# SyncE's queue and the order of seven products in a gated-attention kernel with a feed-forward layer

## The chip, the cores and the metric

The kernel runs on one core of a Trainium2 chip, in one launch. The metric is the device time in microseconds; the numbers below are medians of repeated runs. The engines are called as the profile calls them: PE (TensorE), PEld (its weight loads), DVE (VectorE), ACT (ScalarE), POOL (GpSimd), SP (SyncE). SP computes nothing here; it issues nearly all DMA transfers, one after the other.

## The reference

Two blocks follow each other. The first is attention with a complex gate per step, run as a recurrence over 768 steps for 4 batches of 8 heads of width 48; the second is a feed-forward layer over the 3072 resulting rows of 384 numbers.

```python
scale = np.minimum(mag, 0.999) / (mag + 1e-06)        # mag = |a_re + i a_im|
for t in range(S):
    new_re = ar * S_re - ai * S_im                     # ar, ai: the scaled gate of step t
    new_im = ar * S_im + ai * S_re
    S_re, S_im = new_re + k_t v_t^T, new_im
    y[:, :, t] = q_t S_re
x = y as 3072 x 384
h = x @ w_in                                           # 384 x 2048
out = (h * cos(h)) @ w_out                             # 2048 x 384
```

## The kernel before, in words

The 768 steps of a batch are cut into chunks of 128, and two chunks make a group; with 4 batches there are 12 groups, 0 to 11, and three groups to a batch. Inside a chunk the recurrence becomes matrix products. The running product of the gates is built as powers P and their inverses Q from logarithms (`log_steps`: squares of a_re and a_im on ACT, their sum `lg` on DVE, then a chain of logarithms and exponentials that goes back and forth between ACT and DVE, with tiles `mag`, `rs`, `tan`), from sums over the chunk on PE (`lgs`, in `p_powers`), and from phases (`phs`, in `g_phase`). Keys are multiplied by Q and queries by P (`p_apply`, `g_stack`), and turned from rows to columns: DVE transposes blocks of 32 (`tr`), one transfer stores them to memory (`moved`), and four transfers bring back `kT` and one `qT` (`f_transpose`).

The attention of a group g is `chunks(g)`. For each of its two chunks it yields four steps: two of `f_scores` (four heads each: PE's `sc` and, on DVE, the causal mask into `atm`), `f_state` (PE's `sp`, then DVE adds it to the `state` that the next chunk reads; left out for the last chunk of a batch), and `f_out` (PE's `yp`, from `atm`, the values and, if there is one, the state; ACT copies it to `yT`). Then `f_x` stores `yT` (two transfers, `x<-yT`) and `f_xt` reads it back in the layout that the feed-forward layer needs (one transfer, `xT<-x`); its `late["x"]` keeps these in order. A last step of `chunks` loads k, q and v for the group after next.

The feed-forward layer's first product is `first(g)`: eight blocks `hp`, six matmuls each, followed by ACT's sine (`gate`), ACT's square (`junk`, which only feeds a check) and DVE's product into `gate`. The second product is done for groups 0 and 1 as it stands (`mm2`, stored at L1113), and from group 2 (`PLAIN` is 2) on by seven products of half-size blocks, as Strassen and Winograd have it. `mixed` makes the sums of gate blocks (`s`, four DVE steps), `quarters` and `last_quarter` those of the weights, and `seventh` one product p, in two halves of four matmuls; it evacuates into `ot` and issues the stores (p = 4 and p = 6). PE's rows are named `sum` for products 0, 3, 5, 6 and `op` for 1, 2, 4. The order of the products is that in which `products` lists them:

```python
        return [lambda p=p, part=part: seventh(g, p, part)
                for p in (0, 1, 3, 2, 5, 4, 6)[lo:hi] for part in range(2)]
```

One loop runs the groups: its pass n holds the attention of group n, the seven products of group n - 1, the gate preparation for group n + 1 and the first product of group n. `weave` merges these lists: each list gets a stretch of the pass (0.0 to 0.36, say), its steps are spread evenly over it, and all steps are sorted by place. This fixes PE's order, since every matmul is chained to the one before it. On DVE, ACT and SP the order within the loop is not written out by hand: a planner in the framework orders each engine's instructions when the kernel is built, by their readiness in its own estimate of times, unless `behind(a, b)` ties a behind b. Each engine then runs its list strictly as built.

The last power of a chunk (the `row` of P) goes to memory by `row_out`, and comes back turned, as `end`, by two transfers of `row_back`; `p_end` prepares it on DVE for `state_next`. In the kernel before, `even_steps` issues both as soon as P is ready.

Of the kernel before, what the change touches and what calls it, by code (L numbers as in the profile page):

```python
# [487 lines left out]
def fast_path(ctx, tc, q, k, v, a_re, a_im, moe_w_in, moe_w_out, out, least, odd, wide,  # L488
# [7 lines left out]
    nc = tc.nc  # L496
    B, H, S, D = q.shape
    DM, DF = moe_w_in.shape
    C = 128
    NCH = S // C  # L500
    G = 2
    N = B * NCH
    NG = N // G
# [30 lines left out]
    late = {}  # L534
# [8 lines left out]
    def behind(ins, other):  # L543
        tc.add_manual_dep(ins.ins, other.ins.name, mybir.DependencyInfo(
            mybir.DependencyClass.NoSync, mybir.DependencyReason.DATA))
# [14 lines left out]
    X = [dict() for _ in range(NG)]  # L560
# [6 lines left out]
    def load(g, names, i=None, put=nc.sync.dma_start):  # L567
        for name in names:
            ap = {"re": a_re, "im": a_im, "q": q, "k": k, "v": v}[name]
            if name not in X[g]:  # L570
                X[g][name] = ld.tile([C, G, H, D], F32, tag=name, name=name,
                                     bufs=2 if name == "v" else 1)
            b, c = divmod(g * G + (i or 0), NCH)
            one, n = i or 0, G if i is None else 1
            steps = ap[b].rearrange("h (c p) d -> p c h d", p=C)[:, ds(c, n)]
            tile_ = X[g][name][:, ds(one, n)]
            parts = [(0, C, 0)]
            if name in ("re", "im") and g >= PEG:

                parts = [(0, C - 16, 1), (C - 16, C - 1, 1)]  # L580
                put(out=tile_[C - 1:C], in_=steps[0:1])
            for i_ in range(n):
                for lo, hi, by in parts:
                    put(out=tile_[lo:hi, i_], in_=steps[lo + by:hi + by, i_])
# [101 lines left out]
    def matmul(out, **kw):  # L686
        chain(nc.tensor.matmul(out, **kw), "tensor")  # L687
# [31 lines left out]
    def cut(t, i, n):  # L719
        return (flat(t) if len(t.shape) == 4 else t)[:, ds(i * DM, n * DM)]  # L720
# [91 lines left out]
    def even_steps(g, i, n):  # L812


        x = X[g]
        u = cut(x["mag"], i, n)
        P, Q = cut(x["P"], i, n), cut(x["Q"], i, n)
        ins = [vector.scalar_tensor_tensor(out=u, in0=Q, scalar=HUGE, in1=P,
                                           op0=ALU.min, op1=ALU.mult)]
        yield  # L820
        for t in P, Q:
            ins.append(vector.scalar_tensor_tensor(out=t, in0=u, scalar=3.0, in1=t,
                                                   op0=ALU.subtract, op1=ALU.mult))
            yield

        for one_, what in zip(ins, ("carried", "split")):
            if what in x and g > PEG:
                behind(one_, x[what])
        if g > 0:
            row_out(g, i, n, nc.sync)  # L830
            row_back(g, i, n, nc.sync)

    def row_out(g, i, n, queue):
        P = cut(X[g]["P"], i, n)
        queue.dma_start(out=X[g]["row"][ds(i * DM, n * DM)],
                        in_=P[C - 1:C].rearrange("o x -> (o x)"))

    def row_back(g, i, n, queue):
        row = X[g]["row"][ds(i * DM, n * DM)]
        end = X[g]["end"][:, ds(i * H, n * H)]  # L840
        for a in range(2):
            queue.dma_start(out=end[ds(a * D, D)], in_=row.rearrange("(x d) -> d x", d=D))
# [18 lines left out]
    def g_angle(g, i, n):  # L861

        at = cut(X[g]["tan"], i, n)
        special(out=at, in_=at, func=AF.Arctan)
# [187 lines left out]
    def f_xt(g, i=0, n=G):  # L1052

        if i == 0:
            X[g]["xT"] = msb.tile([C, ND, G, C], F32, tag="xT", name="xT")
        moved = X[g]["moved"].rearrange("p s d g t -> (p s d) g t").rearrange("(c r) g t -> r c g t", r=C)
        put = nc.sync.dma_start(out=X[g]["xT"][:, :, ds(i, n)], in_=moved[:, :, ds(i, n)])
        behind(put, late["x"])
        late["x"] = put

    def mm1_sums(g, jp, i=None):

# [55 lines left out]
    PLAIN, HJ, E2 = 2, NJ // 2, DM // 2  # L1118
# [41 lines left out]
    def seventh(g, p, part):  # L1160


        x, name = X[g], SEVEN[p]
        if p == 0 and part == 0:
            x["sum"] = pm.tile([C, E2], F32, tag="acc", name="sum", bufs=1)
            x["ot"] = [msb.tile([C, DM], F32, tag="ot", name="ot") for _ in range(G)]

        alone = g == NG - 1 and p == 6
        summed = p in (0, 3, 5, 6) and not alone
        if not summed and part == 0:  # L1170
            x["op"] = pm.tile([C, E2], F32, tag="m", name="op", bufs=2)
        ps = x["sum"] if summed else x["op"]
        for j in range(part * HJ // 2, (part + 1) * HJ // 2):
            matmul(ps, lhsT=left(g, name, j), rhs=right[name][:, j],
                   start=(j == 0 and (p == 0 or not summed)),
                   stop=(j == HJ - 1), skip_group_check=summed)
        if part == 0:
            return
        c11, c12, c21, c22 = (x["ot"][i][:, ts(half, E2)] for i in range(2) for half in range(2))
        if g == NG - 1:  # L1180
            c12 = rest
        if p in (0, 3, 5) or p == 6 and not alone:
            late["scalar"] = scalar.mul(out={0: c11, 3: c21, 5: c22, 6: c12}[p], in_=ps, mul=scale)
        if g == NG - 1 and p == 5:
            scalar.mul(out=c12, in_=ps, mul=scale)
        for part_ in {1: [c11], 2: [c21], 4: [c21, c22], 6: [c12] * alone}.get(p, []):
            added = vector.scalar_tensor_tensor(out=part_, in0=ps, scalar=scale,
                                                in1=part_, op0=ALU.mult, op1=ALU.add)
            if alone:
                behind(added, late["read DVE"])  # L1190
            late["vector"] = added
        row = g * G * C
        if g == NG - 1 and p == 1:
            behind(nc.sync.dma_start(out=out[ds(row, C), 0:E2], in_=c11), late["line"])
        elif p == 4:
            put = nc.sync.dma_start(out=out[ds(row + C, C), :], in_=x["ot"][1])
            if g == NG - 1:
                behind(put, late["read SP"])
        elif p == 6 and alone:
            late["store"] = lambda: nc.scalar.dma_start(out=out[ds(row, C), E2:DM], in_=c12)  # L1200
        elif p == 6:
            nc.sync.dma_start(out=out[ds(row, C), :], in_=x["ot"][0])

    def products(g, lo, hi):
        if g < PLAIN:
            return []
        return [lambda p=p, part=part: seventh(g, p, part)
                for p in (0, 1, 3, 2, 5, 4, 6)[lo:hi] for part in range(2)]
# [31 lines left out]
    def powers(g):  # L1240
        return [lambda i=i: p_powers(g, i) for i in range(G)]

    def prods(g):
        if not 0 <= g < NG:
            return
        if g not in (1, 2):
            yield from powers(g)
            yield lambda: g_angle(g, 0, G)
        yield lambda: (g_carry(g), g_split(g))
        yield lambda: (p_even(g, 0, G), p_apply(g, 0, G))  # L1250
# [9 lines left out]
    def chunks(g):  # L1260
        for n in range(g * G, g * G + G):
            for hh in range(2):
                yield lambda n=n, hh=hh: f_scores(n, hh)
            yield lambda n=n: f_state(n)
            yield lambda n=n: f_out(n)
        yield lambda: (f_x(g), f_xt(g))
        if g + 2 < NG:
            yield lambda: load(g + 2, ("k", "q", "v"))

    def first(g):  # L1270
        order = range(NJ // 2) if g < PLAIN else (0, 4, 1, 5, 2, 6, 3, 7)
# [2 lines left out]
    def second(g, i):  # L1274
        return [lambda j0=j0: mm2(g, i, j0, 4) for j0 in range(0, NJ, 4)] if g < PLAIN else []
# [12 lines left out]
    into, back = weight_parts()  # L1288
# [267 lines left out]
    upper = second(1, 0)  # L1556
# [10 lines left out]
    quarters()  # L1567
    for n in range(2, NG):
        weave((mixes(n - 1, 2, 4), 0.0, 0.12), (logs(n + 1), 0.0, 0.02), (chunks(n), 0.0, 0.36),
              (upper[2:] if n == 2 else [], 0.0, 0.2), (products(n - 1, 0, 2 + (n < NG - 1)), 0.0, 0.36),  # L1570
              (prods(n + 1), 0.25, 0.27), (second(n - 1, 1), 0.36, 0.5),
              (products(n - 1, 2 + (n < NG - 1), 7), 0.4, 0.56),
              (phases(n + 1), *((0.472, 0.476) if n == PLAIN else (0.516, 0.524))),
              (keys(n + 1), *((0.5, 0.62) if n == PLAIN else (0.53, 0.64))),
              (last_quarter() if n == PLAIN else [], 0.9, 1.0), (first(n), 0.56, 1.0),
              (mixes(n, 0, 2), 0.9, 1.0), (guarded(n - 1, per) if n > 3 else [], 0.1, 0.9))
# [101 lines left out]
```

## Time and profile before

| what | value |
|---|---|
| runs | 654.09, 654.53, 654.77 us; median 654.53 |
| profiled execution | 653.01 us, of which the span of the profile is 651.2 us |
| PE clock granted | full in all 40 slices |
| PE, PEld | 641.0 us and 576.4 us busy |
| DVE, ACT, POOL | 492.0, 392.8 and 30.9 us busy |
| DMA | 94.90 MB, 146 GB/s in the mean |

The page gives busy times over the whole span. A pass of the loop takes about 50 us: from the first hp of group 3 (204.33 us after the span's start) to that of group 4 it is 51.20 us, and the next ones are 50.24 and 50.32 us long. PE is named with nearly all of the chain of work that ended last (92% of the span). SP's own waits, on the other hand, are long and many: it waits 117.9 us in eight places for ACT to release the tile of a_re, and 52.6 us in seven places for ACT's copy of yT. A wait on SP or an idle stretch on DVE tells nothing by itself; what counts is whether PE waits.

### The profile page before, as it was taken

The numbers are of one execution on the slowest core, as the hardware profiler recorded it, in microseconds if no ns is written. First come the engines' busy times: TensorE is split into PE (matmuls) and PEld (weight loads), VectorE is DVE, ScalarE is ACT, GpSimd is POOL, SyncE is SP. The second block draws the span as 40 slices with busy tenths as digits, with TensorE's granted clock in tenths as the row PEclk, the third lists the DMA queues.
The fourth block names the chain that finished last, engine by engine and source line by source line (L and its number), as shares of the span: only waits on it lengthen the run. The fifth ranks groups of instructions, "written<-read, shape, count | busy, mean of one in ns | idle before, by whom it ended". The sixth has DMA issues, their size and how long they took to land.

```text
span 651.2 us, 10758 instructions
## 1 busy us (share of the span) xinstructions
PE 641.0 (98%) x4075; PEld 576.4 (89%) x4075; DVE 492.0 (76%) x799; ACT 392.8 (60%) x726; POOL 30.9 (5%) x53
## 2 busy tenths in 40 slices
PE   8999999999999999999999999999999999999997
PEld 6888877777999999899899899899899999999996
DVE  6999989888687688786787787876877878862251
ACT  7898687284583593494494485485576476433330
POOL 4010200000000000010010010000000000000000
PEclk9999999999999999999999999999999999999999
DMA  9968755727627656747738737836836843363001
GB/s 249 244 179 203 225 164 123 170 62 182 146 49 182 158 146 148 194 110 167 209 82 191 204 85 167 205 96 151 226 105 146 219 123 98 112 134 120 25 1 31
DMA packets 232920, 94.90 MB, mean 146 GB/s; under 512 B 208701, under 2 KB 221246, under 8 KB 232858
## 3 DMA queue, kind: packets, MB, share of 16 engines
q1 hardware_dynamic: 225320, 68.51, 45.3%
q0 software_dynamic: 5824, 25.50, 11.7%
q8 instruction: 34, 0.56, 0.4%
q10 hardware_dynamic: 1714, 0.11, 0.2%
q14 instruction: 28, 0.23, 0.1%
HBM read 69.28 MB, written 24.81 MB: 144 GB/s over the span
## 4 chain that ended last, share of the span: by engine, by line
PE 92%; ACT 4%; DVE 3%; DMA 0%; issue 0%; SPq 0%; DVEq 0%
PE hp L687 38%; PE op L687 18%; PE sum L687 16%; PE sc L687 6%; PE yp L687 6%; PE sp L687 4%; PE phs L687 2%; PE lgs L687 1%; ACT tan L707 1%; PE yr L687 1%; PE tp L948 1%; ACT rs L707 1%; ACT lg L707 1%; ACT L703 1%; DVE mag L676 1%; DVE atm L676 1%
## 5 line engine op out<-in xcount | busy, mean ns | idle before, releaser
L687 PE MATMUL hp<-xT,w_in 128*128 128x256 f32 (+1 forms) x1176 | 252.5, 375 | 0.0
L687 PEld LDWEIGHTS hp<-xT,w_in 128*128 128x128 f32 x1176 | 219.6, 190 | 30.2 <-issue 0.2
L707 ACT ACTIVATE gate<-hp,half_pi_b 128x512 f32<-128x512 f32 x96 | 66.0, 687 | 118.5 <-PE hp L687 118.5
L687 PE MATMUL op<-w_out,gate 128*128 128x192 f32 (+1 forms) x448 | 100.7, 374 | 0.0
L676 DVE TENSOR_TENSOR gate<-hp,gate 128x512 f32<-128x512 f32 x96 | 65.7, 684 | 45.8 <-ACT junk L676 45.7
L687 PEld LDWEIGHTS op<-w_out,gate 128*128 128x128 f32 x448 | 75.9, 190 | 16.9 <-issue 2.0
L676 ACT ACTIVATE junk<-hp 128x512 bf16<-128x512 f32 x96 | 56.7, 591 | 0.0
L687 PE MATMUL sum<-t_s,s 128*128 128x192 f32 x320 | 56.3, 329 | 0.0
L687 PEld LDWEIGHTS sum<-t_s,s 128*128 128x128 f32 x320 | 52.1, 190 | 1.5 <-issue 1.5
L676 DVE TENSOR_TENSOR atm<-sc,causal 128x512 f32<-128x512 f32 x48 | 32.9, 689 | 23.4 <-PE sc L687 23.4
L687 PEld LDWEIGHTS sc<-qT,kT 96*128 96x128 f32 x384 | 47.4, 192 | 2.3 <-issue 0.6
L687 PE MATMUL sc<-qT,kT 96*128 96x128 f32 x384 | 49.0, 276 | 0.2 <-ACT qT L676 0.2
L676 ACT ACTIVATE ot<-sum 128x192 f32<-128x192 f32 x39 | 12.6, 322 | 53.7 <-PE sum L687 53.4
L676 DVE SCALAR_TENSOR_TENSOR ot<-op,ot 128x192 f32<-128x192 f32 x40 | 13.3, 354 | 38.0 <-PE op L687 36.4
L687 PE MATMUL yp<-atm,v 128*48 128x128 f32 x352 | 33.6, 277 | 0.9 <-ACT Q L707 0.6
L703 ACT ACT_TABLE_LOAD x24 | 30.8, 1283 | 1.2 <-PEq L1662 0.7
L676 ACT COPY yT<-yp 48x512 f32<-48x512 f32 x44 | 25.3, 574 | 7.4 <-PE yp L687 7.0
L687 PE MATMUL yp<-qT,state 96*48 96x128 f32 x304 | 29.7, 272 | 0.0
L687 PE MATMUL sum<-w_out,gate 128*128 128x192 f32 x160 | 29.7, 329 | 0.0
L687 PE MATMUL sp<-v,ks 128*96 128x48 f32 x320 | 29.7, 245 | 0.0
L687 PEld LDWEIGHTS sp<-v,ks 128*96 128x96 f32 x320 | 29.6, 165 | 0.0
L676 ACT CAST tan<-phs 128x384 int32<-128x384 f32 x24 | 11.4, 480 | 29.4 <-PE phs L687 29.4
(147 smaller groups left out, 987.4 us busy)
## 6 DMA issues: line engine op xcount, KB each, us to landing
moved<-tr SPq DMA_DIRECT2D x20, 768.0 KB
raw<-in_moe_w_in_dram POOLq DMA_DIRECT2D x16, 768.0 KB, 5.1
raw<-in_moe_w_out_dram POOLq DMA_DIRECT2D x16, 768.0 KB, 4.6
kT<-moved SPq DMA_DIRECT2D x40, 192.0 KB
qT<-moved SPq DMA_DIRECT2D x10, 768.0 KB
k<-in_k_dram SPq DMA_DIRECT2D x24, 192.0 KB
q<-in_q_dram SPq DMA_DIRECT2D x24, 192.0 KB
v<-in_v_dram SPq DMA_DIRECT2D x24, 192.0 KB
```

What stands on the lines that cost most here:

```text
L676: ins = getattr(self.engine, op)(**kw)
L687: chain(nc.tensor.matmul(out, **kw), "tensor")
L703: chain(nc.scalar.preload_act_table_set(table))
L707: chain(nc.scalar.activation(func=func, **kw))
L948: chain(nc.tensor.transpose(ps[:, h], X[g][name[0] + "s"][:, x0 + h].rearrange("p a d -> p (a d)"), ident), "tensor")
```

## The change

It has five edits, all in the fast path.

- `even_steps` no longer issues row and end for groups above 2. A new step `ends(g)` does it, put at 0.36 of the pass, and the row's transfer is tied behind `X[g - 1]["back"]`, the transfer of xT of the group before.
- `f_xt` keeps its transfer as `X[g]["back"]`.
- The loads of k, q and v for the group after next are tied behind that transfer, and so is the store of product 4.
- In the pass of group 2 the step `prods(3)`, the powers of the third group, moves from 0.25 to 0.3 of the pass. (The diff compares n with `PLAIN`, which is 2.)
- Of the seven products only two, not three, are spread over 0 to 0.36 together with the attention; the other five follow from 0.37 on, and not four from 0.4 on.

```diff
@@ even_steps
-        if g > 0:
-            row_out(g, i, n, nc.sync)
-            row_back(g, i, n, nc.sync)
+        if 0 < g <= PLAIN:
+            ends(g)
+
+    def ends(g):
+        put = row_out(g, 0, G, nc.sync)
+        if g > PLAIN:
+            behind(put, X[g - 1]["back"])
+        row_back(g, 0, G, nc.sync)
@@ row_out
-        queue.dma_start(out=X[g]["row"][ds(i * DM, n * DM)],
-                        in_=P[C - 1:C].rearrange("o x -> (o x)"))
+        return queue.dma_start(out=X[g]["row"][ds(i * DM, n * DM)],
+                               in_=P[C - 1:C].rearrange("o x -> (o x)"))
@@ f_xt
-        late["x"] = put
+        late["x"] = X[g]["back"] = put
@@ seventh
-            if g == NG - 1:
-                behind(put, late["read SP"])
+            behind(put, late["read SP"] if g == NG - 1 else X[g + 1]["back"])
@@ chunks
-            yield lambda: load(g + 2, ("k", "q", "v"))
+            yield lambda: load(g + 2, ("k", "q", "v"), put=lambda **kw: behind(
+                nc.sync.dma_start(**kw), X[g]["back"]))
@@ the loop over the groups
-              (upper[2:] if n == 2 else [], 0.0, 0.2), (products(n - 1, 0, 2 + (n < NG - 1)), 0.0, 0.36),
-              (prods(n + 1), 0.25, 0.27), (second(n - 1, 1), 0.36, 0.5),
-              (products(n - 1, 2 + (n < NG - 1), 7), 0.4, 0.56),
+              (upper[2:] if n == 2 else [], 0.0, 0.2), (products(n - 1, 0, 2), 0.0, 0.36),
+              (prods(n + 1), *((0.3, 0.32) if n == PLAIN else (0.25, 0.27))),
+              ([lambda: ends(n + 1)] if n + 1 < NG else [], 0.36, 0.37), (second(n - 1, 1), 0.36, 0.5),
+              (products(n - 1, 2, 7), 0.37, 0.56),
```

## The prediction

> **What bounds the kernel now.** I read the page's busy table first, then the busy time by stretches, one for each pass of the group loop (a pass runs from the first hidden-layer matmul, hp, of one group to that of the next).
>
> ```profile
> span 651.2 us, 10758 instructions
> PE 641.0 (98%) x4075; PEld 576.4 (89%) x4075; DVE 492.0 (76%) x799; ACT 392.8 (60%) x726; POOL 30.9 (5%) x53
> ```
>
> ```profile
> 100.00:154.00 54.00, 53.12 (x275) 38.85 (x274) 45.34 (x66) 30.52 (x52) 0.00 (x0) 1.00 0.54 128
> 204.33:255.53 51.20, 51.20 (x347) 47.88 (x347) 40.09 (x65) 31.80 (x60) 1.86 (x3) 1.00 0.62 156
> 255.53:305.77 50.24, 50.09 (x332) 46.46 (x331) 38.65 (x62) 31.80 (x60) 1.85 (x3) 1.00 0.63 155
> ```
>
> The first pair in a stretch is its length and PE's busy time. From 154 us on PE has no gap longer than 0.15 us in any pass until the last group. Before that the stretch 100 to 154 holds 0.88 us of idle. So all that a better order could win between 100 and 608 us is 0.88 + 3 x 0.15 = **1.3 us**; the other idle time is the start and the 4.7 us after the last product, and the change touches neither. What remains is the question whether the new order keeps PE fed. Next I read the order of time on PE, DVE and ACT around the attention of group 4 (it begins at 224.88):
>
> ```profile
> 224.88 1.06 PE L687 MATMUL sc<-qT,kT 96*128 96x128 f32 x8
> 225.78 1.47 PE L687 MATMUL sum<-w_out,gate 128*128 128x192 f32 x8
> 227.08 1.06 PE L687 MATMUL sc<-qT,kT 96*128 96x128 f32 x8
> 227.97 1.48 PE L687 MATMUL sp<-v,ks 128*96 128x48 f32 x16
> 229.29 1.53 PE L687 MATMUL sum<-w_out,gate 128*128 128x192 f32 x8
> 230.75 0.43 PE L687 MATMUL yp<-atm,v 128*48 128x128 f32 x4
> ```
>
> ```profile
> 225.98 0.69 DVE L676 TENSOR_TENSOR atm<-sc,causal 128x512 f32<-128x512 f32 x1 [1.49 <-PE sc L687]
> 226.58 0.68 DVE L676 TENSOR_TENSOR gate<-hp,gate 128x512 f32<-128x512 f32 x1
> ...
> 227.84 0.96 DVE L676 TENSOR_TENSOR lg<-lg,tan 128x768 f32<-128x768 f32 x1
> 228.72 0.68 DVE L676 TENSOR_TENSOR atm<-sc,causal 128x512 f32<-128x512 f32 x1
> ...
> 230.97 0.96 DVE L676 SCALAR_TENSOR_TENSOR mag<-re,mag 128x768 f32<-128x768 f32 x1
> 231.85 0.56 DVE L676 TENSOR_SCALAR lg<-lg 128x768 f32<-128x768 f32 x1
> ```
>
> ```profile
> 226.97 0.84 ACT L749 ACTIVATE tan<-im 128x768 f32<-128x768 f32 x1
> ...
> 230.10 0.84 ACT L707 ACTIVATE mag<-lg 128x768 f32<-128x768 f32 x1
> ```
>
> Start and length in us. The readout yp needs both masks (atm), the second only at its middle. The second mask is done at 229.40 and yp starts at 230.75: a margin of 1.35 us, which is just the half product (sum, 1.46 to the next start) between sp and yp. Two DVE steps there start within 0.03 us of ACT's end: lg (227.84, after tan 227.81) and mag (230.97, after ACT's mag 230.94). So they are tied to ACT, not to DVE's load.
>
> **What the Trainium skill says.** "TensorE: Matmul & The Clock Gate", section on the array's architecture: ScalarE's and VectorE's queues are strict FIFO, only PE pulls weight loads ahead. The trace agrees: each DVE row starts after the one before it. "DMA: Bandwidth & Descriptors", Anatomy of one DMA: a semaphore wait is held by the issuing sequencer, so what stands behind it waits too; one DMA costs about 2.0 us and bytes / 436e3 (fitted on GpSimd's path). The trace shows xT issued 2.35 us after the second x has been issued (197.24 to 199.59), for 192 KB each: the same size. "Perfetto Trace Analysis", Identifying the Most-Contended Engine, prefers weight-load busy time to matmul busy time; at 89% against 98% both say PE.
>
> **The change, part by part.** I use the order of instructions of the changed kernel as built.
>
> *Products.* No matmul is added or taken away. Per pass only two half products move on PE: the second half of the first goes from before the first chunk's yp to behind it, and the second half of the second from before the second chunk's scores to behind the second yp; the scores get the first as cover instead. Gain: a half product after sp cost 1.37 us where 1.30 is usual (chain of waits), so 0.07 x 7 = 0.5 us. Loss: the first yp can start at 229.29 instead of 230.75.
>
> *Masks on DVE, which the diff doesn't show.* With the cover gone the built order of DVE also changes. I work out when the second mask ends, on the clock of group 4, with the spacing of starts in the trace (lg 0.88, mask 0.60, a mix step 0.33, mag 0.88, short lg 0.46; 0.06 from DVE's end to PE). Undisturbed, yp's second half starts at 229.29 + 0.95 = 230.24 (0.50 later than the start where the group opens a batch and has no state term).
> - Groups 4, 6, 10: the second mask stands behind mag and lg. mag starts at 230.97, whatever DVE does, so 230.97 + 0.88 + 0.46 = 232.31, mask done 233.00, PE on at 233.06. Loss 2.8 us; 3.3 in group 6, which opens a batch.
> - Groups 5, 7, 8, 9: both masks stand behind lg, the second also behind two mix steps: 227.84 + 0.88 + 0.60 + 0.66 = 229.98, done 230.67, PE on at 230.73. Loss 0.5; 0.95 in group 9, which opens a batch.
> - The second chunk's masks come later too. After ACT's second tan (234.8) come mag, lo, tan, mask, tan, mask: the masks end at 238.1 and 239.6. In group 7 PE wants the last at 239.4: 0.25. Groups 5 and 8 close a batch and have no sp to cover (1.32 us): 1.4 each. Where PE is already 2.8 late there is none.
> - Group 3 keeps its masks early: 0.2 for lo. Group 11 keeps its order: 0.
>
> Sum: 2.8 + 2.8 + 3.3 + (0.5 + 1.4) x 2 + 0.75 + 0.95 + 0.2 = 14.6 us; less the 0.5, **14.1**. Bounds: 9 if only the three mag groups count; 17 if each of the eight groups loses 0.3 more on the way to PE.
>
> *The pass of group 2.* Before, the four lgs matmuls ran while PE waited for the masks; now they stand behind yp. The masks end as before (139.83 and 141.29), so lgs adds its own **0.86 us** (238.45 to 239.31 in group 4).
>
> *SyncE's queue.* x and xT now come before row, end and the loads: x goes some 2 to 3 us earlier. That is worth nothing, since no hp waited for xT. But in the pass of group 2 the built order is x, x, store of group 1's second tile, xT. The store waits for ACT's copy of a product that ends right before hp:
>
> ```profile
> 145.99 0.80 SPq L1048 DMA_DIRECT2D x<-yT  x2
> ...
> 149.25 0.38 SPq L1057 DMA_DIRECT2D xT<-x  x1
> ...
> 154.64 0.61 SPq L1113 DMA_DIRECT2D out_dram<-ot  x1
> ```
>
> The store starts at 154.64, 0.6 us after hp began. With xT behind it, and behind xT all six loads and the row, hp gets its input at: store 0.6 after the product's end, 0.6 to issue, 0.1, then xT (384 KB) 2.0 + 0.9 = 2.9 by the skill's fit, an estimate: **4.2 us** of PE. Bounds: 3.2 (2 us for xT) and 5.9 (4.6, the time from xT's issue at 199.59 to an hp at 204.16 that did not wait).
>
> *row and end, later.* row now stands behind the v loads, end between the two moved stores. Next to wait: p_end on DVE, which is moved behind the third or fourth gate, where DVE sits idle for 1.0 us ahead of the fourth gate of a pass (at 267.34): 0. But 1,536 four-byte packets stand in front of the second moved, and so of kT and qT. qT's issue ended 5.6 us before sc (270.49 to 276.09) without a wait. I take 0, for a delay falls in front of waits already counted; upper bound 1 us in 8 groups. The stores behind xT and the loads' hold cost 0: they have 20 us and more until their tile is wanted.
>
> **Sum.** 14.1 + 0.86 + 4.2 = 19.2 us on the profiled execution's 653.01 (span 651.2 and 1.8 around it) gives 672.2; the median of the runs, 654.53, is 1.5 above that execution: **673.7**.
>
> **Rivals.**
> - *Only the queue and the short waits cost* (0.15): DVE gets past mag and lg before PE needs the mask, because ACT's chain starts earlier than I think. For it: DVE has 24% idle. Against it: two rows tied to ACT within 0.03 us. 14.6 - 8.9 + three short waits of 0.6 = 7.5, less 0.5, with 0.86 and 4.2: 12.1, or 666.6.
> - *qT comes late* (0.14): the four-byte packets hold up kT and qT. Up to 0.7 us in 8 groups on top: 679.3. Against it: in most groups sc shows no wait at all.
> - *Faster* (0.03): the one mechanism is the better cover. PE keeps no gap if the second mask ends by 25.9 us after the pass's first hp (230.2 in group 4) and xT lands before hp. Then 0.5 and at most 1.3 are won: 652.7. It needs the masks at least 2.8 us earlier than the built order lets them be.
> - *The change does next to nothing* (0.03): the stated move is mostly nominal, two half products a pass, and the queue's new order hides; 654.5.
>
> **Numbers.** My own case has 0.65 and says 673.7. The range reaches down to the first rival with a smaller xT wait and up to the second: 662 to 681. Slower by over 0.2% (1.3 us, about what a measurement can tell) takes 0.65 + 0.15 + 0.14 = 0.94.
>
> **What would show it.** PE's waits should name yp waiting for DVE atm, some 13 to 15 us in all, three of them near 2.8; one wait of about 4 us of hp for the transfer of xT near 155; the stretches with the attention of groups 4, 6 and 10 near 54 us, with that of 7 near 52. Wrong if PE stays at 98% or if the hp near 155 starts without a gap: then the built order is not what decides, or the store leaves earlier than its copy lets it.

## The result and the profile after

| kernel | median of the runs | profiled span | PE busy | PE idle in the span |
|---|---|---|---|---|
| before | 654.65 us (654.03 to 655.56) | 651.2 | 641.0 | 10.2 |
| after | 678.73 us (677.28 to 680.3) | 677.0 | 650.2 | 26.8 |

The change makes the kernel slower: the ratio is 1.0368, with a 95% interval of 1.0351 to 1.0385. The span grew by 25.8 us. Subtracting the table's columns splits it into two parts: PE is idle 16.6 us longer, and PE is *busy* 9.2 us longer although it runs the same 4,075 matmuls. The first is waits, the second for the most part a lower clock. The busy table of the page shows the second number, and the clock row, of 40 slices of 16.9 us, shows where to look for it (three digits below 9):

```profile
span 677.0 us, 10782 instructions
PE 650.2 (96%) x4075; PEld 582.3 (86%) x4075; DVE 493.1 (73%) x799; ACT 393.5 (58%) x726; POOL 31.5 (5%) x53
PEclk9999999997999989999979999999999999999999
```

PE's waits in the kernel after, with the total, the number of times and the longest. Before, the yp line for atm read 0.3 us and the hp line did not exist:

```profile
PE yp L687 <- DVE atm L676: 10.5, 14, 2.9
PE hp L687 <- DMA xT<-x: 4.5, 1, 4.5
...
PE lgs L687 <- DVE lo L676: 1.0, 3, 0.6
...
PE sc L687 <- DMA qT<-moved: 0.8, 1, 0.8
```

The busy time by stretches; the rows answer to those of before: up to the first hp behind the attention of group 2, then the passes with the attention of group 4 and of group 5.

```profile
100.00:159.20 59.20, 53.12 (x275) 38.60 (x273) 49.78 (x70) 31.24 (x53) 0.00 (x0) 0.98 0.44 111
212.86:268.40 55.54, 53.02 (x347) 49.42 (x347) 40.38 (x65) 31.88 (x60) 1.87 (x3) 0.97 0.59 143
268.40:320.50 52.10, 50.64 (x332) 46.41 (x331) 38.75 (x62) 31.75 (x60) 1.85 (x3) 1.00 0.62 152
```

The second row is worth a pause. The pass is 4.34 us longer than the 51.20 us of before. 2.52 us of that is idle (55.54 - 53.02); the other 1.82 us is PE busy for longer (53.02 against 51.20), at a clock of 0.97. The order of time on PE in that pass, and below it DVE's:

```profile
236.50 1.48 PE L687 MATMUL sp<-v,ks 128*96 128x48 f32 x16
238.38 0.43 PE L687 MATMUL yp<-atm,v 128*48 128x128 f32 x4 [0.40 <-DVE atm L676]
...
241.59 0.43 PE L687 MATMUL yp<-atm,v 128*48 128x128 f32 x4 [2.11 <-DVE atm L676]
...
242.28 0.51 PE L687 MATMUL yp<-qT,state 96*48 96x128 f32 x4
242.72 1.65 PE L687 MATMUL sum<-w_out,gate 128*128 128x192 f32 x4
```

```profile
236.44 0.95 DVE L676 TENSOR_TENSOR lg<-lg,tan 128x768 f32<-128x768 f32 x1
...
237.64 0.68 DVE L676 TENSOR_TENSOR atm<-sc,causal 128x512 f32<-128x512 f32 x1
...
239.50 0.96 DVE L676 SCALAR_TENSOR_TENSOR mag<-re,mag 128x768 f32<-128x768 f32 x1 [0.84 <-ACT mag L707]
240.38 0.55 DVE L676 TENSOR_SCALAR lg<-lg 128x768 f32<-128x768 f32 x1
240.85 0.68 DVE L676 TENSOR_TENSOR atm<-sc,causal 128x512 f32<-128x512 f32 x1
```

No half product stands between sp and yp any more. The second mask stands behind mag and the short lg, and mag waits for ACT with DVE idle 0.84 us in front of it. Right after the 2.11 us gap, the matmuls themselves stretch: four yp matmuls take 0.51 us where 0.39 is usual, and four sum matmuls take 1.65 us where eight took 1.47. That is the clock. The same stretches in slices of 2 us (the third number from the end is the granted clock):

```profile
156.00:158.00 2.00, 0.00 (x0) 0.00 (x0) 2.00 (x3) 0.00 (x0) 0.00 (x0) 0.77 0.64 193
158.00:160.00 2.00, 0.80 (x2) 0.71 (x3) 1.80 (x1) 0.00 (x0) 0.00 (x0) 0.50 1.19 286
160.00:162.00 2.00, 2.00 (x6) 1.55 (x6) 0.00 (x0) 0.00 (x0) 0.00 (x0) 0.50 1.25 231
162.00:164.00 2.00, 2.00 (x7) 1.61 (x6) 0.00 (x0) 0.00 (x0) 0.00 (x0) 0.52 1.32 257
...
242.00:244.00 2.00, 2.00 (x18) 1.69 (x13) 2.00 (x5) 2.00 (x4) 0.00 (x0) 0.60 0.04 8
244.00:246.00 2.00, 2.00 (x10) 2.00 (x9) 2.00 (x3) 1.56 (x5) 0.00 (x0) 0.54 0.66 124
```

A third such stretch follows the 2.89 us wait in group 6 (348 to 355). For part of these stretches PE was idle and lost nothing. PE's busy time in each 2 us slice from 156 to 356 us, times one less the clock, adds up to 6.9 us: three quarters of the 9.2. The other 2.3 us are not the clock: the third row of the stretches above, at a clock of 1.00, has 50.64 us of PE where before has 50.09. They fit the waits themselves, as an estimate from the rows above: a run of four yp matmuls is 0.39 us long but the next starts 0.22 us after it, so each wait lays bare up to 0.17 us of an end that otherwise lies under the next start. That was not measured apart.

In SyncE's queue, the three lines shown of before are now:

```profile
144.04 0.89 SPq L1053 DMA_DIRECT2D x<-yT  x2
155.32 0.36 SPq L1118 DMA_DIRECT2D out_dram<-ot  x1
155.85 0.38 SPq L1062 DMA_DIRECT2D xT<-x  x1
```

x goes 1.95 us earlier than before, and xT 6.60 us later, behind the store. PE's hp starts at 159.20, 2.97 us after xT's issue ended (156.23).

### The profile page after: what moved, and what is told of

The parts are those of the page before. It is cut to its first block, busy times and chain, and to the rows that moved or that the text cites. A ratio compares the mean times of both kernels' runs of the same rounds, so it can differ in the third digit from the quotient of the medians.

```text
span 677.0 us, 10782 instructions
## 1 busy us (share of the span) xinstructions
PE 650.2 (96%) x4075; PEld 582.3 (86%) x4075; DVE 493.1 (73%) x799; ACT 393.5 (58%) x726; POOL 31.5 (5%) x53
## 4 chain that ended last, share of the span: by engine, by line
PE 78%; ACT 11%; DVE 6%; DMA 2%; issue 2%; ACTq 0%; SPq 0%; DVEq 0%
PE hp L687 36%; PE op L687 16%; PE sum L687 13%; PE yp L687 4%; PE sc L687 3%; PE phs L687 2%; PE sp L687 2%; ACT L703 2%; ACT rs L707 2%; DVE tan L676 2%; ACT tan L707 1%; DVE mag L676 1%; ACT lg L707 1%; DVE atm L676 1%; ACT mag L707 1%
## 5 line engine op out<-in xcount | busy, mean ns | idle before, releaser
L687 PEld LDWEIGHTS yp<-atm,v 128*48 128x48 f32 x352 | 19.0, 123 | 17.1 <-DVE atm L676 12.8
L687 PE MATMUL sum<-w_out,gate 128*128 128x192 f32 x160 | 32.7, 352 | 0.0
L687 PE MATMUL yp<-qT,state 96*48 96x128 f32 x304 | 29.8, 273 | 0.0
```

## The experiments

The theory after the result: three things cost. The place of the masks on DVE (waits of about 10 us), xT behind the store (4.5), and a half clock behind the long gaps (about 7). The rivals: that the products' move costs by itself, since it takes away PE's cover; that the queue's late row, end and loads cost by themselves; and that DVE's late work only moves from one wait to another. Every experiment was measured beside the kernel before on the same chip; "above before" is the difference of the two medians. The last two columns compare profiles: how much longer PE is busy and idle than in before's.

| kernel | us | above before | ratio, 95% interval | PE busy | PE idle |
|---|---|---|---|---|---|
| after | 678.73 | 24.1 | 1.0351 to 1.0385 | +9.2 | +16.6 |
| e1, after, store tied behind xT | 672.52 | 16.6 | 1.0239 to 1.0273 | +6.2 | +11.9 |
| e2, before, xT late | 663.14 | 7.2 | 1.0089 to 1.0128 | +4.0 | +6.3 |
| e3, products alone | 662.15 | 6.2 | 1.0065 to 1.0113 | +1.8 | +7.7 |
| e4, queue alone | 670.01 | 14.1 | 1.0198 to 1.0232 | +2.8 | +13.9 |
| e5, products, DVE as before | 659.16 | 2.8 | 1.0034 to 1.0067 | +0.8 | +5.8 |
| e6, queue, store tied | 665.47 | 9.1 | 1.0112 to 1.0165 | +4.1 | +9.5 |
| e7, after, first masks early | 687.63 | 31.2 | 1.0443 to 1.0505 | +15.7 | +19.2 |
| e8, e7 and last mask late | 686.25 | 29.8 | 1.0421 to 1.0487 | +15.6 | +17.7 |
| e9, after, DVE as before, store tied | 660.19 | 4.3 | 1.0048 to 1.009 | +0.1 | +6.0 |
| e10, queue, DVE as before, store tied | 659.05 | 3.1 | 1.0028 to 1.0062 | +0.4 | +5.7 |

### xT behind the store: undone (e1), and alone (e2)

e1 is the changed kernel with one tie more:

```diff
-            nc.sync.dma_start(out=out[ts(g * G + i, C), :], in_=ot)
+            put = nc.sync.dma_start(out=out[ts(g * G + i, C), :], in_=ot)
+            if g == 1 and i == 1:
+                behind(put, X[g + 1]["back"])
```

> The changed kernel with one tie more: the store of group 1's second tile goes behind xT of group 2 in SP's queue. If the store in front of xT costs PE its whole wait (4.5 us in the profile after) and the half-clock stretch that follows it (hp took 23.3 us there and 20.7 elsewhere, 2.6 us), the time falls by about 7.1 us to 671.6, the hp wait is gone and the mean granted clock rises. If the half-clock stretch has another cause, it falls by 4.5 us to 674.2. If xT is late for another reason (the loads, the row), it stays at 678.7.

e2 is the kernel before with xT of group 2 tied behind that store, and nothing else (not printed here: for the tie, the step that issues this xT is listed at 0.5 of the pass):

```diff
+        if g == 2:
+            behind(put, late["mm2"])          # in f_xt; late["mm2"] is the store of group 1's second tile
```

> The kernel before, with one thing changed: xT of group 2 is issued behind the store of group 1's second tile, as the changed kernel does it, and all else stays. If that wait and its clock loss are a cause by themselves, the time rises by 4.5 + 2.6 = 7.1 us to 661.8, with one hp wait of about 4.5 us and a stretch of half clock of some 6 us. If the clock falls only because of many short waits elsewhere, it rises by 4.5 to 659.2 and the clock stays full.

e1 came to 16.6 us above before, 7.5 less than after. The hp wait and the half clock from 157 to 164 us are gone from its profile. e2 came to 7.2 above. Both differences are well over the wait itself, which e2 shows alone:

```profile
158.64 23.79 PE L687 MATMUL hp<-xT,w_in 128*128 128x256 f32 x96 [4.46 <-DMA xT<-x]
```

96 hp matmuls took 20.88 us in before and take 23.79 here: 4.46 us of wait and 2.9 us of slower matmuls behind it, 7.4 together (a second wait for xT, of 0.87 us, comes at 467). So this gap cost about 1.65 times its length. That factor is not fixed: in e4 below, the same wait of 4.58 us was followed by a shorter half clock (hp took 22.64 us), and cost about 6.3 us, 1.4 times its length. Both expectations had the mechanism.

### The products alone (e3), and the queue alone (e4)

e3 is the kernel before with the products' lines of the change; e4 is the change without them, so it has the queue's edits and the later powers of the third group.

```diff
-              (products(n - 1, 0, 2 + (n < NG - 1)), 0.0, 0.36),
+              (products(n - 1, 0, 2), 0.0, 0.36),
-              (products(n - 1, 2 + (n < NG - 1), 7), 0.4, 0.56),
+              (products(n - 1, 2, 7), 0.37, 0.56),
```

> The kernel before with the move of the products alone (two in 0 to 0.36, five from 0.37); row, end, loads and stores as before. In this build DVE keeps both first-chunk masks ahead of mag. If what costs is where DVE has the masks, and the queue's new order is what moved them, yp waits at most some tenths a group: 654 to 656. If the lost half product between sp and yp costs by itself, as the prediction had it (the second mask stands late because the cover is gone), the waits of groups 4 to 10 come with it: 11 us of waits, 665 or more.

> The changed kernel with the products' places of before: queue edits and the later powers of the third group alone. In this build the second mask stands behind mag in groups 4, 6, 7, 9 and 10, with the half product still between sp and yp. If the queue edits move the masks, yp waits 2.8 - 1.4 = 1.4 us in 4, 7 and 10 and 1.9 in 6 and 9, 8 us in all, and the xT wait with its clock loss (7.1) and the 0.7 of group 2 stay: about 670. If the move of the products is the cause of the mask waits, only xT and group 2 are left: about 662.5.

e4 came to 670.0 us, as expected if the queue's edits move the masks. In it the products stand where they stood in before, and still the second mask of group 4 comes behind mag and the short lg:

```profile
238.28 0.96 DVE L676 SCALAR_TENSOR_TENSOR mag<-re,mag 128x768 f32<-128x768 f32 x1 [0.84 <-ACT mag L707]
239.16 0.55 DVE L676 TENSOR_SCALAR lg<-lg 128x768 f32<-128x768 f32 x1
239.62 0.68 DVE L676 TENSOR_TENSOR atm<-sc,causal 128x512 f32<-128x512 f32 x1
```

```profile
240.36 0.43 PE L687 MATMUL yp<-atm,v 128*48 128x128 f32 x4 [1.21 <-DVE atm L676]
```

DVE's order is set by the planner when the kernel is built, so here an edit of SyncE's queue has changed the built order of DVE. How the planner weighs the transfers is not shown. PE's wait is 1.21 us here, against 0.40 + 2.11 = 2.51 in the kernel after: the 1.30 us of difference are the half product that stands between sp and yp in e4.

The products alone cost 6.2 us, a result between the two that were expected, and by neither of their ways. From 154 us on, no yp waits for a mask. In six of the passes lgs waits for lo, 5.2 us in all, and once, in group 10, sc waits 1.43 us for qT, although SyncE issues its transfers in the order of before:

```profile
286.43 1.48 DVE L676 TENSOR_TENSOR atm<-sc,causal 128x512 f32<-128x512 f32 x2
287.82 0.55 DVE L676 TENSOR_SCALAR raw<-raw 128x768 uint32<-128x768 uint32 x1
288.29 0.95 DVE L676 TENSOR_TENSOR mag<-mag,tan 128x768 f32<-128x768 f32 x1
289.16 0.95 DVE L676 SCALAR_TENSOR_TENSOR lo<-lg,hi 128x768 fp32r<-128x768 f32 x1
```

```profile
288.60 0.44 PE L687 MATMUL lgs<-hi,exact 128*128 128x384 f32 x1
290.16 0.45 PE L687 MATMUL lgs<-lo,exact 128*128 128x384 f32 x1 [1.12 <-DVE lo L676]
```

Both masks of the second chunk stand ahead of lo ("x2" in one row). In before, one of them stood behind it. That suggested e5.

### The products with DVE's order of before (e5)

e5 is e3 with one tie more:

```diff
+        if n > 2 * G and n % G and hh and n + 1 < NG * G:
+            behind(y["masked"], X[n // G + 1]["turned"])      # "turned" is the step tan<-mag,tan
```

> The five products behind the attention alone (before's queue), with DVE's order given back to before's: in the attention of groups 3 to 10 the second mask of the second chunk is tied behind the step tan<-mag,tan, so that mag, lo and tan go ahead of it. Theory A (the 6.2 us of the products alone are DVE's order: both masks ahead of lo, and PE's lgs waits for lo): the lgs waits go, and with them 5.2 us; the time lies within 1.5 us of before, possibly 0.5 below it. Theory B (a half product less between sp and yp costs PE's cover as such, whatever DVE's order): 5 us or more stay, as waits of yp for atm.

3.5 us of the 6.2 went, 2.8 stayed. What stayed is lgs waiting for lo in the same six passes, now 0.57 to 0.68 us each, 3.7 us in all, and the wait for qT in group 10, now 1.09 us:

```profile
289.25 0.44 PE L687 MATMUL lgs<-lo,exact 128*128 128x384 f32 x1 [0.68 <-DVE lo L676]
```

Before lgs, PE now has one half product less in the pass (1.3 us), so it gets there earlier than lo does. So neither theory had it whole: most of the 6.2 was DVE's order, the rest is lost cover, but in front of lgs and not of yp.

### The queue with the store tied (e6)

e4 with the tie of e1.

> The queue's edits alone (products where before has them), with the store of group 1's second tile tied behind xT of group 2. The queue alone cost 14.1 us, of which 4.6 us are the wait of hp for xT and about 1.7 us the half clock that followed it. Theory A (only a PE gap of 2 us and more is followed by a half clock; gaps of 1.2 and 1.7 us are not): no half clock is left before the last product, the masks' waits of 1.2 to 1.7 us stay: 7.8 us above before. Theory B (any gap lowers the clock): half clocks appear after the gaps near 240, 343, 396 and 499 us, and the time is 11 us or more above before.

It came to 9.1 above before: between the theories, and the claim that gaps under 2 us leave the clock alone fell. In e6 the clock was halved behind the gaps of 1.20 + 0.38 us near 140 and of 1.66 us near 339, and not behind the gaps of 1.22 near 235 and of 1.66 near 496:

```profile
142.00:144.00 2.00, 2.00 (x15) 1.64 (x12) 0.00 (x0) 0.84 (x2) 0.00 (x0) 0.50 0.63 116
...
236.00:238.00 2.00, 2.00 (x19) 1.81 (x16) 2.00 (x5) 2.00 (x5) 0.00 (x0) 1.00 0.03 9
...
340.00:342.00 2.00, 2.00 (x8) 2.00 (x7) 1.83 (x4) 2.00 (x4) 0.00 (x0) 0.50 0.08 12
...
498.00:500.00 2.00, 2.00 (x19) 2.00 (x19) 2.00 (x3) 1.96 (x5) 0.00 (x0) 1.00 0.47 88
```

e4, with the same gaps of 1.66 us, kept the full clock behind both. The runs of e6 are also spread over 5.3 us (662.88 to 668.21), those of e4 over 0.8.

### The masks put early in the changed kernel: two attempts that failed (e7, e8)

e7 is e1 with lg tied behind the first mask and mag behind the second; for that, the steps of the logarithm were listed later, at 0.062 of the pass. e8 adds the tie of e5.

```diff
+        if g > 3:
+            behind(added, Y[(g - 1) * G][0])       # added: lg<-lg,tan
+            behind(folded, Y[(g - 1) * G][1])      # folded: mag<-re,mag
-        (logs(n + 1), 0.0, 0.02)
+        (logs(n + 1), *((0.062, 0.082) if n > 2 else (0.0, 0.02)))
```

> The changed kernel with the store of group 1's second tile tied behind xT of group 2, and with the first chunk's masks put ahead of lg and mag on DVE in groups 3 to 10 (lg tied behind the first mask, mag behind the second; the logarithm's steps begin at 0.062 of the pass). Theory A (waits add up stage by stage): the 4.5 us of xT, the first chunk's 8.9 us of mask waits and all 8 us of half clock go; the second chunk's masks stand ahead of lo as with the products alone, 5 to 6 us; with 0.9 us of lgs in the pass of group 2 it is 6 to 8 us above before. Theory B (the delay of DVE only moves to another wait): more than 12 us above before.

> The kernel of e7 with the second chunk's second mask tied behind tan<-mag,tan as well, which gives DVE before's order in the attention. Theory A: only 0.9 us of lgs behind yp in the pass of group 2 and about 1 us of qT in group 10 remain, less 0.5 us for the shorter cover: 0 to 2 us above before. If the new place of the products and of the queue has a gain of its own, it shows here: 0.5 us or more below before. Theory B (what is left is the queue, not DVE's order): more than 4 us above before.

Both are slower than the change itself, by rival B's way: the delay moved on. The first chunk's waits are down to 0.32 us in group 4 and 0.76 in groups 6 and 9, but lgs waits twice in seven passes. In e7:

```profile
PE lgs L687 <- ACT hi L728: 8.3, 7, 1.9
PE lgs L687 <- DVE lo L676: 5.7, 8, 0.9
PE yp L687 <- DVE atm L676: 3.6, 6, 1.2
```

DVE's order of time in e7 tells why:

```profile
231.14 0.95 DVE L676 TENSOR_TENSOR lg<-lg,tan 128x768 f32<-128x768 f32 x1
232.01 0.68 DVE L676 TENSOR_TENSOR atm<-sc,causal 128x512 f32<-128x512 f32 x1
234.97 0.56 DVE L676 TENSOR_SCALAR raw<-raw 128x768 uint32<-128x768 uint32 x1 [2.28 <-DMA raw<-in_moe_w_in_dram]
235.45 0.55 DVE L676 SCALAR_TENSOR_TENSOR state<-sp,state 96x384 f32<-96x384 f32 x1
235.91 0.94 DVE L676 SCALAR_TENSOR_TENSOR mag<-re,mag 128x768 f32<-128x768 f32 x1
```

The later listing changed DVE's order in two ways. lg stands behind four mix steps and the mask (231.14; ACT's square for it had ended at 229.77), and raw, a step that checks a weight, came in front of mag and waited 2.28 us for its transfer. ACT's mag had ended at 233.93, so mag is 1.98 us late. The chain of logarithms has no such slack: hi starts 12.9 us after the first sc, 10.0 in before. The two gaps of each pass were then followed by a half clock in six passes, which makes 13.4 of the 15.7 us that PE is busy longer. e8 has the same delays, so its own tie tells nothing.

### DVE's order of before in the changed kernel (e9), and in the queue alone (e10)

The steps of the logarithm stay at the start of the pass, and every tie is set from the mask's side:

```diff
+            if n % G == 0:
+                behind(X[n // G + 1]["ahead"][hh], y[hh])       # lg behind mask 1, mag behind mask 2
+            elif hh == 0:
+                behind(X[n // G + 1]["times"], y[hh])           # mag<-mag,tan behind mask 3
+            else:
+                behind(y[hh], X[n // G + 1]["turned"])          # mask 4 behind tan<-mag,tan
...
+            if p == 3 and 2 < g + 1 < NG - 1:
+                behind(step, Y[(g + 1) * G][1])                 # last mix steps behind mask 2
```

The condition that keeps the mask ties between the second chunk of group 2 and group 10 is not printed here. e9 has this and the tie of e1; e10 is e9 with the products where before has them.

> The changed kernel with the store of group 1's second tile tied behind xT of group 2, and with DVE's order in the attention of groups 3 to 10 put back to that of before by ties (first mask ahead of lg, second ahead of mag and of the last four mix steps, the second chunk's first mask ahead of mag<-mag,tan, its last behind tan<-mag,tan), while the logarithm's steps begin where the change has them, at the start of the pass. Theory A (the changed queue costs only by the place of the masks and of xT; the products cost 0.6 to 0.7 us of lgs in six groups, as e5 left): waits of yp for atm at most 0.4 us from 200 us on, no hp wait, no or one half clock; 3.5 us above before (2.75 of e5 and 0.9 of lgs in the pass of group 2). Theory B (the queue's later row, end and loads have a cost of their own): more than 8 us above before. Theory C (the delay only moves, as in e7): lgs waits for hi on ACT, over 12 us above before.

> The kernel of e9 with the products where before has them: so only the queue's new order is left, without xT behind the store and with the masks early. Theory A (the order of SyncE's queue costs nothing but by what it does to the masks and to xT): within 1.5 us of before, with 0.7 us more wait than before near 140 us and under 1.5 us of qT. Theory B (a cost of its own by late row, end or loads): the 9 us that e6 left stay in good part, over 4 us above before.

The changed kernel falls from 24.1 to 4.3 us above before, with every transfer and product but one store still in the place that the change gave it. The second mask of group 4 is back in front of mag:

```profile
229.61 0.96 DVE L676 TENSOR_TENSOR lg<-lg,tan 128x768 f32<-128x768 f32 x1 [0.17 <-ACT tan L749]
230.48 0.68 DVE L676 TENSOR_TENSOR atm<-sc,causal 128x512 f32<-128x512 f32 x1
...
232.73 0.96 DVE L676 SCALAR_TENSOR_TENSOR mag<-re,mag 128x768 f32<-128x768 f32 x1 [0.77 <-ACT mag L707]
```

In e9's profile no yp waits for a mask after 142 us, and PE is busy as long as in before (641.1 us): there is no half clock left but at the end.

```profile
PE lgs L687 <- DVE lo L676: 4.3, 6, 0.9
PE yp L687 <- DVE atm L676: 1.6, 2, 1.4
```

The first row is the cover lost in front of lgs, as in e5, the second lies in the pass of group 2 (139 and 142 us; before it waited 0.88 there, for a mask and for ACT). e10, without the products' move, is 3.1 above before, outside the 1.5 that was expected, under the 4 of the rival. Its new waits are scattered: 1.57 us of yp near 139 to 142, 0.76 of yp at 446, 1.2 of sum for ACT, 1.0 of lgs in the start and 0.7 of qT. Only the last names a transfer, and e3 and e5 wait longer for qT with the queue of before. So what the 3.1 us come from stays open. Which single edit of e4, the later powers of the third group included, makes the planner move the masks is open too: no run takes them apart. No version beat before, and before leaves 1.3 us to win in the loop.

## Why the prediction was right, and where its steps were not

The time was forecast as 673.7 us and came to 678.73, inside the range, on the side and by the two mechanisms named. That it came so near is in part luck: two errors in the sum stood against each other. PE is idle 16.6 us longer where waits of 19.7 were forecast, and it is busy 9.2 us longer where 0.5 less was.

| step | predicted | measured in the kernel after |
|---|---|---|
| group waits: 4, 6, 10 | 2.8, 3.3, 2.8 | 2.51, 2.89, 0.22 |
| 5, 8 | 1.9, 1.9 | 1.28, 1.46 |
| 7, 9, 3 | 0.75, 0.95, 0.2 | 0.42, 0.62, 0.58 |
| sum of these | 14.6 | 10.0 |
| xT behind the store | 4.2 | 4.51 |
| pass of group 2 | 0.86 | 0.70 (waits of 1.20 + 0.38, before 0.59 + 0.29) |
| qT, row and end | 0, at most 1 in 8 groups | 0.76 in group 10 |
| half product after sp | gain of 0.07 a pass, 0.5 | 0.07 where no wait follows (e9: 51.13 for 51.20) |
| lower clock | not in the sum | 6.9 of the 9.2 that PE is busy longer |

- **The masks' waits** in groups 4 and 6 were sized right: two DVE rows tied to ACT's end, read off the trace of before, set PE's start to about 0.4 us. e9 shows that they are the cause: with the masks back in front of mag, these waits go.
- **Group 10** is the term that failed, by 2.6 us. Its attention has no loads, so its list has one step less, and at that spacing the half product still lands between sp and yp (sum at 558.09, yp at 559.55). The order of PE in that pass was taken to be as in group 4. Besides, sc starts 0.76 us late there, for qT, while DVE and ACT go on. The waits of groups 5, 7, 8 and 9 were 0.3 to 0.6 us too large each.
- **xT** was sized right, 4.2 for 4.51. The estimate from the Trainium skill ("DMA: Bandwidth & Descriptors", Anatomy of one DMA) gave 2.9 us for 384 KB; from the end of the issue to hp it took 2.97, on a queue other than the one that the page's fit was made on.
- **The lower clock** is missing from the sum. A gap of PE was priced at its length; at 4.5 us it cost 7.4 (e2) and 6.3 (e4). The full clock of before in all slices hid this price. The Trainium skill states the mechanism ("TensorE: Matmul & The Clock Gate", Part 1: The HAM clock gate): after an idle window of about 3.4 us the array's clock is halved, and the window runs free. Here gaps shorter than that window sufficed, see below.
- **Why the masks moved** was told wrong. "With the cover gone the built order of DVE also changes" puts it down to the products. e4 shows the queue's edits doing it with the products unmoved, and the products alone leave the first chunk's masks early (e3). The missing half product adds only its 1.3 us to the waits in groups 4 and 6 (1.21 and 1.66 us in e4, 2.51 and 2.89 after), but this takes them past 2 us, where the clock goes too. So the parts do not add: 6.2 + 14.1 = 20.3 alone, 24.1 together.
- **"The scores get the first as cover instead"** missed a place. A half product went from in front of lgs as well, worth 0.6 to 0.7 us in six passes (e5). In the kernel after it is mostly hidden: PE has already waited for a mask, so lo is in time.
- **row, end, loads and stores at 0.** No run speaks against it. In e9, which carries all of these edits, PE's waits over 0.15 us from 154 us on are the six of lgs for lo and none for a transfer. qT came late once in the kernel after, by 0.76 us in group 10; but e3 and e5, with the queue of before, wait 1.43 and 1.09 us at the same place, so row and end need not be the reason.

- **The rivals.** "Only the queue and the short waits cost" fell with the waits of 2.5 and 2.9 us in groups 4 and 6; "qT comes late" showed in one group of eight, and e3 and e5 have that wait without its reason, the later packets of row and end; "faster" and "next to nothing" have nothing for them in the profile.

## What to carry to other kernels

Where a planner orders the engines, an edit of a queue can cost by what it does to an engine that it does not touch: compare the built order of every engine, and hold the critical steps by ties from the side of the consumer that PE waits for. A step pulled ahead on an in-order engine pushes another one back; the chain that it delays must be followed to where PE meets it next (masks against lo, in e3 and e7). Price a gap of the matmul engine by its length and by the slower matmuls behind it. Where busy time grows by several microseconds with an unchanged number of matmuls, look at the clock; a growth of 1.8 us came in e3 without any half clock before the last product.

## What the runs showed of the hardware

The clock of PE fell to half behind gaps much shorter than the idle window of about 3.4 us that the Trainium skill gives ("TensorE: Matmul & The Clock Gate", Part 1: The HAM clock gate). Taking together the waits within 3 us, from 130 us on: every gap of 1.7 us and more of total idle, in the kernel after and in e1, e2, e4, e7 and e8, was followed by a half clock (1.03 + 0.86, 0.40 + 2.11, 2.89, 4.46 to 4.58 among them). Of those between 1.2 and 1.7 us some were and some were not, with the same gap at the same place differing between kernels: 1.20 + 0.38 near 140 us halved the clock in e6 and not in after or e4; 0.80 + 0.69 near 406 did in e7, and 0.86 + 0.69 did not in e8. None of 1.1 us or less was. The half clock lasted 3.4 us behind the 2.11 us gap of after and 6.8 us behind those of 2.89 and 4.51 us; in e4 it lasted 3.4 us behind a gap of 4.58.

The clock changes on a raster. In every trace, each half stretch from 130 us to the last product is 3.41 or 6.83 us long, and their starts within a trace lie whole multiples of 3.41 us apart: 157.08, 242.42 and 348.23 us in after (25 and 31 steps), 294.70, 352.73 and 407.34 in e7 (17 and 16 steps). This fits the free-running window of that page, and the pair near 406 us fits it too: the two gaps of e7 fall into one step (403.93 to 407.34, PE busy for 1.92 us of it), those of e8 into two (busy for 2.53 and 2.74). Chance seems to have a part in it: the six runs of e6, one and the same kernel, have mean clocks from 0.999 (662.88 us) down to 0.991 (668.21), and the longer runs have the lower clocks. The idle time in a step is not the whole rule: of two steps of e6 in which PE was busy for 1.75 us (336.19 to 339.60) and 1.76 (493.20 to 496.62), the first was followed by a half clock and the second was not. No run here moved a gap on the raster and left all else, so what decides there is not shown.
